# Another order for the first seven inner products of a float32 matrix kernel

## The chip, the cores and the metric

The kernel runs on one core of a Trainium2 chip. The metric is the device time of one execution in microseconds (us). An instruction that the profile calls PE ran on TensorE, PEld is TensorE's weight load, DVE is VectorE, ACT is ScalarE, POOL is GpSimd, and SP is the queue from which the kernel issues its loads.

## What is computed

The inputs are float32: x is 2048 x 1024, the two parts of a Fourier matrix over the sequence are 2048 x 2048, the two over the hidden dimension 1024 x 1024, w1 is 1024 x 3584 and w2 is 3584 x 1024.

```python
g = sigmoid((x * gate_w).sum(-1, keepdims=True))
a = einsum("bsd,ed->bse", x, dft_hid_re)
b = einsum("bsd,ed->bse", x, dft_hid_im)
y = einsum("ts,bse->bte", dft_seq_re, a) - einsum("ts,bse->bte", dft_seq_im, b)
h = relu(einsum("bsd,df->bsf", x, w1) + b1) ** 2
out = g * y + (1 - g) * (einsum("bsf,fd->bsd", h, w2) + b2)
```

The change lies in the very first product of the first line with a matrix: x with the hidden Fourier matrix (`x_stage`).

## The kernel before, in words

**Float32 by three matmuls.** TensorE works on operands that are split in two: `hi` is the operand rounded by a copy on ScalarE (L220), `lo` is what is left, made by a subtraction on VectorE (L230). One float32 product is hi·hi + hi·lo + lo·hi, three matmuls (L306). A block is a tile of 128 partitions by 2 x 512 elements (512 KB).

**Seven products for eight, at two levels.** Every large product is cut into 2 x 2 blocks and done with seven products of sums of blocks instead of eight (`FACTORS`, `SUMS_L`, `SUMS_R`: left sums S1 to S4, right sums T1 to T4, each one `tensor_tensor` on VectorE, L172). In `x_stage`, five of the seven outer products are again done by seven inner ones (`twice`). In what follows l00 to l11 are the left inner blocks of the very first outer product, r00 to r11 the right ones. The inner products are 1 = l00·r00, 2 = l01·r10, 3 = S4·r11, 4 = l11·T4, 5 = S1·T1, 6 = S2·T2, 7 = S3·T3, with S1 = l10 + l11, T1 = r01 - r00, S2 = S1 - l00, T2 = r11 - T1, S3 = l00 - l10, T3 = r11 - r01, S4 = l01 - S2, T4 = r10 - T2. Each is one step: 24 matmuls, 12 for each of two result tiles.

**Where results go.** PSUM holds four tiles of 128 x 2 x 512, so two steps can hold accumulators at a time. Products 1, 6, 7 and 4 form `chain`, one pair of accumulators that goes on from product to product: after 1 ScalarE copies it out (`put`, L596), after 6 and after 7 VectorE adds it into the block where it belongs (`add`, L603), after 4 ScalarE copies it. Products 5 and 3 form `other`, the second pair. Product 2 (`last`) needs the result of product 1 added: before it starts, ScalarE copies that result from memory back into its accumulators (`prepare`, L293, two copies), and `put` copies the sum out. A matmul that goes on in an accumulator waits until the copy or the add that reads it is done.

**What sets the order.** A loop goes over all steps of the kernel. For each it first emits loads, then the finished `later` work, then sums and `hi` copies of operands that are needed within three steps (`SUMS`) and `lo` parts within two (`RESTS`), then the step's matmuls and what takes its results out. Operands are loaded and made in the order in which the steps need them. A list scheduler puts the instructions of each engine in their final order, the earlier emitted first among those that it takes to be ready; each engine then runs its own in that order.

In the very first outer product the inner order is 1, 5, 3, 6, 2, 7, 4, in all others 5, 1, 3, 6, 2, 7, 4. The operands of product 1 are loaded in pieces ahead of the loop, and 44 small matmuls (`WARM`) run while they land.

## Time and profile before

| | |
|---|---|
| median of 3 runs | 1891.17 us (1890.40 to 1892.99) |
| the profiled execution, its own time | 1888.96 us |
| its span, first to last instruction | 1886.9 us |
| PE busy | 1876.6 us (99%) |
| DVE busy | 1610.3 us (85%) |
| ACT busy | 1001.3 us (53%) |
| DMA | 442.93 MB, mean 235 GB/s |

Busy time is the union of an engine's instructions. In a timeline, a row gives the start from the span's beginning, the duration (of several merged instructions together, with their count), engine, line, operation, and out<-in by the names in the program; what stands in brackets is the idle time before it and what ended it. A matmul row is longer than the distance to the next one, since matmuls overlap.

### The profile page before, as it was taken

The page shows a single profiled execution, that of the slowest core. Times are in us where ns is not written, and L with a number is a line of the kernel's source. Part 1 is how long each engine was busy: PE and PEld are TensorE (multiplying, and loading weights), DVE is VectorE, ACT ScalarE, POOL GpSimd, SP SyncE. Part 2 cuts the span into 40 slices and gives each one's busy share as a digit, 9 for nine tenths or more (in the row PEclk, how much of TensorE's full clock was granted, in tenths as well). Part 3 has the DMA queues.
Part 4 walks back from the last instruction along what each step waited for, and adds up shares of the span by engine and source line. Part 5 has one row for each costly group of instructions (what it writes and reads, how often), then busy time and mean ns, then how long its engine had stood idle before and what let it go on. Part 6 is the DMA issues. An engine that isn't in the chain of part 4 may idle for free.

```text
span 1886.9 us, 21962 instructions
## 1 busy us (share of the span) xinstructions
PE 1876.6 (99%) x8288; PEld 1551.3 (82%) x8288; DVE 1610.3 (85%) x1543; ACT 1001.3 (53%) x1123; POOL 86.8 (5%) x161
## 2 busy tenths in 40 slices
PE   9999999999999999999999999999999999999998
PEld 7888888888888888888888888888888888888887
DVE  8997898599777998798896997989976997789882
ACT  6474564363343554455484797767954434264440
POOL 0000110000010000000000000000100001000000
PEclk9999999999999999999999999999999999999999
DMA  5732989339786489383551865628872887629971
GB/s 223 247 121 86 348 288 412 129 117 375 261 312 256 151 322 383 139 312 112 170 198 56 325 228 195 228 84 299 293 259 97 317 336 265 218 103 370 409 300 45
DMA packets 128425, 442.93 MB, mean 235 GB/s; under 512 B 14128, under 2 KB 23616, under 8 KB 128320
## 3 DMA queue, kind: packets, MB, share of 16 engines
q1 hardware_dynamic: 106416, 363.26, 53.0%
q0 software_dynamic: 21472, 77.61, 10.3%
q8 instruction: 65, 1.06, 0.2%
q10 hardware_dynamic: 432, 0.66, 0.1%
q14 instruction: 40, 0.33, 0.1%
HBM read 362.83 MB, written 78.65 MB: 234 GB/s over the span
## 4 chain that ended last, share of the span: by engine, by line
PE 97%; DVE 2%; ACT 0%; DMA 0%; issue 0%; SPq 0%; DVEq 0%; ACTq 0%
PE ps L306 97%; DVE lo L230 1%; DVE h L603 0%; DVE sum L172 0%; DMA raw<-in_w 0%; DVE o L818 0%; ACT u L596 0%; ACT hi L220 0%; DVE o L820 0%; DVE raw L172 0%; SPq L152 0%; DVEq L172 0%; DVEq L230 0%; ACTq L596 0%
## 5 line engine op out<-in xcount | busy, mean ns | idle before, releaser
L306 PE MATMUL ps<-hi 128*128 128x512 f32 x2328 | 905.7, 390 | 4.0 <-ACT hi L220 3.6
L306 PE MATMUL ps<-lo,hi 128*128 128x512 f32 x2328 | 905.3, 389 | 0.0
L306 PE MATMUL ps<-hi,lo 128*128 128x512 f32 x2328 | 904.2, 389 | 0.1
L220 ACT ACTIVATE hi<-raw 128x1024 fp32r<-128x1024 f32 (+2 forms) x413 | 420.6, 1037 | 399.0 <-DVE raw L172 274.1
L230 DVE TENSOR_TENSOR lo<-raw,hi 128x1024 fp32r<-128x1024 f32 (+2 forms) x413 | 484.5, 1199 | 57.5 <-ACT hi L220 31.3
L306 PEld LDWEIGHTS ps<-hi 128*128 128x128 f32 x2328 | 437.2, 188 | 95.9 <-ACT hi L220 4.2
L306 PEld LDWEIGHTS ps<-hi,lo 128*128 128x128 f32 x2328 | 437.1, 188 | 92.0 <-DVE lo L230 1.0
L306 PEld LDWEIGHTS ps<-lo,hi 128*128 128x128 f32 x2328 | 437.3, 188 | 91.0 <-DVE lo L230 0.4
L172 DVE TENSOR_TENSOR raw<-raw 128x1024 f32<-128x1024 f32 (+1 forms) x276 | 326.4, 1207 | 56.4 <-DMA raw<-in_ct 19.4
L220 ACT ACTIVATE hi<-sum 128x1024 fp32r<-128x1024 f32 (+1 forms) x172 | 176.1, 1036 | 184.8 <-DVE sum L172 151.2
L306 PE MATMUL ps<-hi,both 128*128 128x512 f32 x840 | 259.8, 389 | 0.0
L230 DVE TENSOR_TENSOR lo<-sum,hi 128x1024 fp32r<-128x1024 f32 (+1 forms) x172 | 203.3, 1198 | 32.9 <-PE ps L306 16.6
L306 PEld LDWEIGHTS ps<-hi,both 128*128 128x128 f32 x840 | 157.7, 188 | 33.8 <-ACT ps L293 0.7
L306 PE MATMUL ps<-lo,both 128*128 128x512 f32 x420 | 163.5, 389 | 0.0
L172 DVE TENSOR_TENSOR sum<-raw 128x1024 f32<-128x1024 f32 (+1 forms) x116 | 121.9, 1066 | 35.4 <-PE ps L306 28.1
L172 DVE TENSOR_TENSOR sum<-raw,sum 128x1024 f32<-128x1024 f32 (+2 forms) x87 | 96.8, 1119 | 12.0 <-PE ps L306 11.7
L603 DVE TENSOR_TENSOR h<-h,ps 128x1024 f32<-128x1024 f32 x92 | 98.2, 1086 | 9.6 <-ACT u L596 7.1
L596 ACT ACTIVATE u<-ps 128x1024 f32<-128x1024 f32 x76 | 71.9, 950 | 62.0 <-PE ps L306 54.3
L306 PEld LDWEIGHTS ps<-lo,both 128*128 128x128 f32 x420 | 78.8, 188 | 16.1
L293 ACT ACTIVATE ps<-u 128x1024 f32<-128x1024 f32 (+1 forms) x74 | 70.0, 953 | 22.2 <-DVE o L831 12.0
L700 ACT ACTIVATE h<-h,b1c 128x512 f32<-128x512 f32 x112 | 74.3, 712 | 6.3 <-DVE h L603 6.0
L220 ACT ACTIVATE both<-sum 128x512 fp32r<-128x512 f32 x60 | 37.1, 625 | 52.7 <-DVE sum L172 33.4
(61 smaller groups left out, 650.5 us busy)
## 6 DMA issues: line engine op xcount, KB each, us to landing
raw<-in_ct SPq DMA_DIRECT2D x151, 512.0 KB, 6.2
raw<-h SPq DMA_DIRECT2D x132, 512.0 KB, 7.3
raw<-in_x SPq DMA_DIRECT2D x107, 512.0 KB, 5.3
raw<-in_w SPq DMA_DIRECT2D x98, 512.0 KB, 6.3
raw<-ab SPq DMA_DIRECT2D x72, 512.0 KB, 6.8
h<-h POOLq DMA_DIRECT2D x48, 512.0 KB, 5.7
raw<-in_w1a SPq DMA_DIRECT2D x36, 512.0 KB, 5.0
ab<-ab POOLq DMA_DIRECT2D x32, 512.0 KB, 6.7
```

Of the source, the lines that this page charges most:

```text
L172: nc.vector.tensor_tensor(self.slot[:, k, c], src[0][:, k, c], src[1][:, k, c], op=self.op)
L220: nc.scalar.activation(self.hi[:, k, c], self.block.slot[:, k, c], AF.Copy)
L230: nc.vector.tensor_tensor(self.lo[:, k, c], self.block.slot[:, k, c], self.hi[:, k, c].bitcast(F32), op=SUB)
L293: nc.scalar.activation(t[:, :n, :], b.slot[:, at:at + n, :], AF.Copy, scale=self.sign)
L306: nc.tensor.matmul(self.ps[r // self.per][:, r % self.per, :], a[:, kk, r * P:(r + 1) * P], b[:, kk, :], start=self.at == 1 and kk + n == ...
L596: nc.scalar.activation(view(near.slot, k), view(ps, k), AF.Copy, scale=float(sign))
L603: nc.vector.tensor_tensor(view(near.slot, k), view((src or dst)[k].slot, k), view(ps, k), op=ADD if sign > 0 else SUB)
L700: nc.scalar.activation(dst.slot[:, k, :], (dst.slot if ps is None else ps)[:, k, :], AF.Relu, bias=b1c[:, tile0 + k:tile0 + k + 1])
```

## The change

In the very first outer product alone (`if not steps`), the inner order becomes 1, 2, 5, 3, 6, 7, 4. Product 2 no longer has product 1's result copied into its accumulators: ScalarE copies product 2 out to a tile of its own (`two`), and one step later (`JOIN`) VectorE adds that tile to product 1's result, in two instructions. All later outer products keep their order and their way with product 2.

```diff
-LATER = 3
+LATER, JOIN = 3, 1
...
+            def two(rp, ps):
+                k = 0, 0, rp
+                t = Near("u")
+                nc.scalar.activation(view(t.new(), k), view(ps, k), AF.Copy)
+
+                def join():
+                    add(new, k, t.slot)
+                    t.drop()
+
+                later.append((now[0] + JOIN, join))
+
-            if old and not onto_old:
+            if not steps:
+                last = Group(rows, 1, (two, 2, [new[0, 0, rp] for rp in range(2)]))
+            elif old and not onto_old:
                 last = Group(rows, 1, takes(False, 0, 0, ends))
             else:
                 last = Group(rows, 1, (lambda rp, ps: put(new, (0, 0, rp), ps, ends, sign), 0,
                                        [new[0, 0, rp] for rp in range(2)]),
                              onto=[new[0, 0, rp] for rp in range(2)], sign=sign)
-            begin = ((5, other), (1, chain))
-            for p2, group in (*(begin if steps else begin[::-1]), (3, other), (6, chain), (2, last), (7, chain),
-                              (4, chain)):
+            if steps:
+                turns = (5, other), (1, chain), (3, other), (6, chain), (2, last), (7, chain), (4, chain)
+            else:
+                turns = (1, chain), (2, last), (5, other), (3, other), (6, chain), (7, chain), (4, chain)
+            for p2, group in turns:
                 l_, r_ = FACTORS[p2]
                 step(l2.operand(l_, rows * P), r2.operand(r_), group)
```

## The prediction

> **What bounds the kernel now.** I read the page first, for where TensorE stands idle.

> ```profile
> span 1886.9 us, 21962 instructions
> PE 1876.6 (99%) x8288; PEld 1551.3 (82%) x8288; DVE 1610.3 (85%) x1543; ACT 1001.3 (53%) x1123; POOL 86.8 (5%) x161
> L306 PE MATMUL ps<-hi 128*128 128x512 f32 x2328 | 905.7, 390 | 4.0 <-ACT hi L220 3.6
> ```

> TensorE is busy for all but about 10 us, and of the idle time that its groups show, 3.6 us ended with a `hi` copy. Nearly all of that is at one place, the gap after product 1. The timeline of TensorE's first 20 us shows it, and the windows around it give the clock (PEclk is the third column from the end):

> ```profile
> 10.03 1.07 PE L306 MATMUL ps<-lo,hi 128*128 128x512 f32 x4
> 10.94 1.07 PE L306 MATMUL ps<-hi,lo 128*128 128x512 f32 x4
> 14.91 0.80 PE L306 MATMUL ps<-hi 128*128 128x512 f32 x1 [2.91 <-ACT hi L220]
> 18.38 0.39 PE L306 MATMUL ps<-hi 128*128 128x512 f32 x1
> 18.61 0.39 PE L306 MATMUL ps<-lo,hi 128*128 128x512 f32 x1
> ...
> 12.00:14.60 2.60, 0.00 (x1) 0.00 (x0) 2.60 (x4) 2.60 (x4) 0.00 (x0) 1.00 1.03 419
> 14.60:18.00 3.40, 3.09 (x7) 2.16 (x8) 3.40 (x4) 3.40 (x5) 0.00 (x0) 0.50 1.02 407
> 18.00:21.40 3.40, 3.40 (x17) 2.81 (x16) 3.40 (x4) 3.40 (x4) 0.00 (x0) 1.00 1.01 398
> ```

> Four matmuls take 10.94 - 10.03 = 0.91 us, 0.227 each, so a step of 24 takes 5.44. Product 1's last four start at 10.94; the next could start at 10.94 + 0.91 = 11.85 and starts at 14.91, 3.06 late. Its first eight then take until 18.38, 3.47 where 8 x 0.227 = 1.81 would do, since the granted clock is 0.50 from 14.6 to 18.0: another 1.66. The gap is worth 3.06 + 1.66 = **4.72 us**, and this is all that the change can win.

> What held product 5 back is read from the two engines that make its operands:

> ```profile
> 8.64 2.35 DVE L172 TENSOR_TENSOR sum<-raw 128x1024 f32<-128x1024 f32 x2
> 10.99 1.23 DVE L230 TENSOR_TENSOR lo<-sum,hi 128x1024 fp32r<-128x1024 f32 x1
> 12.13 1.22 DVE L172 TENSOR_TENSOR sum<-raw 128x1024 f32<-128x1024 f32 x1
> 13.80 1.06 ACT L220 ACTIVATE hi<-sum 128x1024 fp32r<-128x1024 f32 x1
> ```

> S1 is the sum at 12.13 (l11, its second block, is the fifth load); its `hi` ends at 14.86 and TensorE goes on. Product 2 needs no sum.

> Then I asked whether VectorE has room for TensorE to run earlier. From its first sum to 99 us it has none:

> ```profile
> 8.64:99.01 90.37, 87.46 (x379) 71.64 (x378) 89.28 (x80) 53.50 (x55) 4.43 (x8) 0.98 0.67 240
> ...
> DVE lo L230 <- ACT hi L220: 0.4, 1, 0.4
> DVE ab L603 <- PE ps L306: 0.4, 1, 0.4
> ```

> The third group is VectorE: busy 89.28 of 90.37 us, with two waits of 0.4. That alone could be work done ahead. The places where TensorE takes the result show whether it is:

> ```profile
> 80.48 1.22 DVE L603 TENSOR_TENSOR ab<-ab,ps 128x1024 f32<-128x1024 f32 x1
> 95.31 3.71 DVE L230 TENSOR_TENSOR lo<-sum,hi 128x1024 fp32r<-128x1024 f32 x3
> ...
> 81.85 0.62 PE L306 MATMUL ps<-hi 128*128 128x512 f32 x2
> 98.17 0.39 PE L306 MATMUL ps<-hi 128*128 128x512 f32 x1
> 99.30 0.39 PE L306 MATMUL ps<-hi,lo 128*128 128x512 f32 x1
> ```

> The add that frees an accumulator ends at 80.48 + 1.22 = 81.70 and the second matmul of the 81.85 row, the first into that accumulator, starts at 82.08: 0.4 to spare. The last of the three `lo` ends at 95.31 + 3.71 = 99.02 and the matmul that reads it starts at 99.30: **0.3 to spare**. Of the three, two belong to the next step and fill the time until the third one's `hi` is made; nothing else had been done ahead there. So at 99 us TensorE stands where VectorE's whole work since 8.64 lets it, and the early gap is paid for out of time that VectorE needs.

> **The change part by part.**

> *The start.* Product 2's blocks now take the third and fourth place among the loads. These two issues and what the DMA view says of each, and of the fifth:

> ```profile
> 2.60 0.44 SPq L152 DMA_DIRECT2D raw<-in_w  x1
> 3.08 0.97 SPq L152 DMA_DIRECT2D raw<-in_x  x2
> ...
> raw<-in_w SPq DMA_DIRECT2D x1, 512.0 KB, 5.7
> raw<-in_x SPq DMA_DIRECT2D x1, 512.0 KB, 6.5
> raw<-in_x SPq DMA_DIRECT2D x1, 512.0 KB, 8.0
> ```

> They land at 2.60 + 5.7 = 8.3 and 3.08 + 6.5 = 9.6, the fifth at about 3.55 + 8.0 = 11.5 (it is the second in the row at 3.08, half of its 0.97 later). ScalarE takes 1.06 and VectorE 1.22 for each: `hi` at 9.4 and 10.7, `lo` at 10.6 and 11.9. Product 2 can start at 11.85 with all but its third kind of matmul, and that comes 0.45 later. I count the whole 4.72 as won here. The same loads cost VectorE: its first instruction behind product 1's own moves from 8.64 to 9.4, and three of them end at 13.1 (T1 waits for the fifth load, 11.5, and for the two `lo`), where the `lo` at 10.99 ended at 12.2: **+0.9 for everything behind**.

> *The joins.* They are new `tensor_tensor`s of 128 x 1024 from two tiles in memory, the shape of the sums. In a queue without a gap such an instruction costs the distance between starts:

> ```profile
> 41.25 1.22 DVE L603 TENSOR_TENSOR u<-u,ps 128x1024 f32<-128x1024 f32 x1
> 42.39 1.22 DVE L230 TENSOR_TENSOR lo<-raw,hi 128x1024 fp32r<-128x1024 f32 x1
> 43.52 1.22 DVE L172 TENSOR_TENSOR sum<-sum,raw 128x1024 f32<-128x1024 f32 x1
> 44.66 1.22 DVE L603 TENSOR_TENSOR u<-u,ps 128x1024 f32<-128x1024 f32 x1
> ...
> 43.77 0.39 PE L306 MATMUL ps<-hi 128*128 128x512 f32 x1
> ...
> L293 ACT ACTIVATE ps<-u 128x1024 f32<-128x1024 f32 x2 | 2.1, 1026 | 0.0
> ```

> Three distances are 3.41, so 1.137 each and **+2.27** for two. ScalarE loses the two copies into PSUM, 2.1 us; product 2's copies out stay. ScalarE was busy 53.50 of the 90.37 us, so its gain is worth at most VectorE's one wait on it, 0.4. The other wait, on TensorE, goes too once VectorE is later: **-0.8** together. The joins themselves are waited for by nobody before the next outer product; what is queued behind them is every `lo` from product 6 on.

> *The order 6, 7, 4.* Product 2 stood between 6 and 7 and gave VectorE 5.44 us for the adds that free `chain`; now product 7 follows at once. Ahead of the first of these adds the code emits 23 VectorE instructions: the two `lo` of product 2, eight sums, ten `lo`, two joins and one sum of the next outer product. From 11.98 (the second `lo`'s end), the add is the 24th: 11.98 + 22 x 1.137 = 37.0. TensorE, 4.72 earlier, would want product 7 at 11.85 + 4 x 5.44 = 33.6. It waits 3.4. Product 7's own add, six instructions on, ends at 43.8, where product 7 would be done at 37.0 + 5.44 = 42.4: 1.4 more. Product 4 so starts at 43.8. The nearest row of before, the add that freed the same accumulator, is the one at 41.25; it ended at 42.5, and product 4 began in the row at 43.77. By 44 us the whole gain is given back.

> *From there to 99 us.* VectorE is later by 0.9 + 2.27 - 0.8 = 2.4, with the same work before it. TensorE meets it with 0.3 to spare: **2.4 - 0.3 = +2.1 us**. The ends: if the two `lo` that belong to the next step are moved behind the one waited for, 2.27 less, -0.2; if neither wait goes and VectorE loses one more 1.06 for a `hi` at the start, +4.0. I take +2.1, since the queue's order follows the same rule. Behind 99 us I count nothing: VectorE's share of the span is 85%, so it gets ahead again.

> *The clock.* A stop of 3.06 us was followed by 3.4 us at 0.50. The stop at product 7 is about as long, so it may cost up to 1.66 there; that is hidden, since VectorE sets the end anyhow. [...]

> The profiled execution would take 1888.96 + 2.1 = 1891.1. It lies 2.2 under the median; on the median's footing **1893.3 us**, 0.11% more. About 0.2%, 3.8 us, is what a measurement of this kernel can tell from no change, so this forecast counts as no change.

> **The rivals.** *Slower: VectorE comes to wait for TensorE.* The adds of products 6 and 7 stand in VectorE's queue at a fixed place. If TensorE is late for one (half clock after its stop), VectorE stands still with all `lo` behind it, for up to half a product, 2.72. Then the end moves by 2.1 + 2.72 = 4.8, 1896.0; with the half clock again after a second stop between 82 and 99 us 6.5, 1897.7. It decides once VectorE's waits on TensorE before 99 us pass 1.7 in sum. For it: 6, 7, 4 in a row and a stop of the length that halved the clock. Against: VectorE's only such wait before was 0.4.

> *Faster: VectorE's queue finds the room.* An order that puts the adds ahead of sums that are needed later would keep the start's gain: -4.72, 1886.4. Against it stands the row at 95.31: at 99 us nothing is ahead.

> *It doesn't do what it says.* If product 2's operands come late the gap stays; VectorE is still 2.4 later, and the time is the forecast's.

> **How the numbers follow.** Forecast 0.55, of which 0.10 above 3.8; slower rival 0.35, of which 0.02 below; faster rival 0.06, of which 0.05 beyond 3.8; no effect at the start 0.04. That gives faster 0.05, same 0.45 + 0.02 + 0.01 + 0.04 = 0.52, slower 0.43. The forecast's own range is 1891.0 to 1895.2. The range given reaches down to 1889.5 for the runs' own spread of 1.3 below and above, and up to 1898.0 for the slower rival; outside stay the faster rival and worse than 6.7.

> **What would show it.** Right: product 2 starts near 11.9 without a wait at a full clock; two joins of 1.2 between 20 and 30 us; TensorE waits on VectorE by 45 us for most of 4.7; VectorE busy as before to 99; the step that began at 98.17 begins near 100. Wrong: TensorE still ahead of the old times at 110 us, or waits of VectorE on TensorE.

## The result, and the profile after

| | before | after |
|---|---|---|
| median of 22 runs each | 1890.39 us | 1894.68 us |
| lowest and highest | 1889.34, 1892.99 | 1892.96, 1896.06 |
| after / before | | 1.0021 [1.0015, 1.0027] |
| the profiled execution, its own time | 1888.96 us | 1895.16 us |

The change costs about 4 us (0.21% of 1890.4; 2.8 to 5.1 by the interval), where +2.1 was forecast. The two profiled executions stand 6.2 us apart, since before's lies 1.4 under its median and after's 0.5 above. What follows explains the profiles, so some 2 us of their difference belongs to these two executions and not to the change.

To see where the time went I set each matmul of after against the one with the same number of before. The distance of their starts, after minus before, is called the shift below; negative means that after is ahead. It moves at few places:

| place | shift, us |
|---|---|
| product 2, once both kernels run at a full clock again | -4.8 |
| most of product 5 | -3.8 |
| most of product 3 | -3.0 |
| first matmul of product 7 (37.75 us) | -0.6 |
| product 4 (45 us) | +1.2 |
| the next outer product's matmul of 85.48 us | +3.6 |
| from 90 us on | +5.3 |
| end | +6.2 |

The gain comes, is gone by 38 us, and two losses follow. Between 90 us and the end little happens but a step of 0.8 at 690 us, where TensorE waits for one `lo`. It belongs to this execution: three of the kernels below have such a step of 0.7 to 1.0 near 285 us and none at 690. TensorE's timeline of the changed kernel:

```profile
10.83 1.07 PE L306 MATMUL ps<-hi,lo 128*128 128x512 f32 x4
11.74 0.39 PE L306 MATMUL ps<-hi 128*128 128x512 f32 x1
...
37.75 0.73 PE L306 MATMUL ps<-hi 128*128 128x512 f32 x2 [2.29 <-ACT hi L220]
...
85.48 0.73 PE L306 MATMUL ps<-hi 128*128 128x512 f32 x2 [2.28 <-ACT hi L220]
```

The row at 11.74 has no bracket: product 2 starts behind product 1 without a wait, and the stop of 2.91 us is gone. Two stops stand in its place, 2.29 us ahead of product 7 and 2.28 us at 85.48. The windows around them (PEclk is the third column from the end):

```profile
33.00:38.46 5.46, 3.17 (x14) 2.31 (x13) 5.46 (x6) 4.24 (x4) 0.00 (x0) 1.00 0.40 138
38.46:41.87 3.41, 3.41 (x10) 2.62 (x9) 2.68 (x3) 0.00 (x0) 0.00 (x0) 0.50 0.21 87
...
82.50:86.25 3.75, 1.47 (x7) 0.91 (x6) 3.75 (x4) 1.71 (x2) 0.49 (x1) 1.00 0.94 294
86.25:89.66 3.41, 3.41 (x9) 2.64 (x8) 3.41 (x4) 0.00 (x0) 0.57 (x2) 0.50 0.92 374
```

Each stop is followed by 3.41 us at a granted clock of 0.50, which costs TensorE 1.7 us. Before had one stop and one such stretch, after has two of each. VectorE's timeline of the changed kernel shows the joins, the adds of products 6 and 7, and what it does ahead of 85 us:

```profile
9.13 2.50 DVE L230 TENSOR_TENSOR lo<-raw,hi 128x1024 fp32r<-128x1024 f32 x2 [1.02 <-ACT hi L220]
11.54 3.49 DVE L172 TENSOR_TENSOR sum<-raw 128x1024 f32<-128x1024 f32 x3
...
21.77 1.22 DVE L603 TENSOR_TENSOR u<-u 128x1024 f32<-128x1024 f32 x1
...
24.04 1.22 DVE L603 TENSOR_TENSOR u<-u 128x1024 f32<-128x1024 f32 x1
...
36.53 1.21 DVE L603 TENSOR_TENSOR u<-u,ps 128x1024 f32<-128x1024 f32 x1
...
42.63 1.22 DVE L603 TENSOR_TENSOR u<-u,ps 128x1024 f32<-128x1024 f32 x1 [1.49 <-PE ps L306]
...
45.38 1.22 DVE L603 TENSOR_TENSOR u<-u,ps 128x1024 f32<-128x1024 f32 x1 [0.39 <-PE ps L306]
...
83.12 1.21 DVE L172 TENSOR_TENSOR sum<-raw 128x1024 f32<-128x1024 f32 x1
```

And the same chain at the second stop, in before (VectorE's sum, then ScalarE's `hi` of it):

```profile
79.35 1.22 DVE L172 TENSOR_TENSOR sum<-raw 128x1024 f32<-128x1024 f32 x1
...
80.60 1.06 ACT L220 ACTIVATE hi<-sum 128x1024 fp32r<-128x1024 f32 x1 [1.21 <-DVE sum L172]
```

ScalarE's row of the same `hi` in after:

```profile
84.37 1.06 ACT L220 ACTIVATE hi<-sum 128x1024 fp32r<-128x1024 f32 x1 [1.21 <-DVE sum L172]
```

In before that `hi` ended at 80.60 + 1.06 = 81.66 and the matmul in the row at 81.85 read it. In after the same sum starts at 83.12, 3.77 later, and the matmul at 85.48 is 3.63 later. The matmul starts 2.50 behind the sum's start in before and 2.36 in after: TensorE had 0.14 us to spare there and is later by the rest. So the second stop is VectorE's queue, though the bracket names ScalarE's `hi`.

VectorE's start, below, is its first three instructions behind product 1's own: two sums and a `lo` in before, which end at 12.21, and the two `lo` of product 2 and T1's sum in after, which end at 12.76. The windows from there to this sum say what the 3.77 consist of. The first line is of before, the second of after; VectorE is the third group:

```profile
12.21:79.35 67.14, 64.44 (x277) 52.94 (x278) 66.17 (x60) 41.57 (x43) 2.30 (x4) 0.97 0.59 214
```

```profile
12.76:83.12 70.36, 67.31 (x285) 53.74 (x283) 68.35 (x62) 39.09 (x40) 2.30 (x4) 0.98 0.57 208
DVE u L603 <- PE ps L306: 1.9, 2, 1.5
```

The start is 0.55 later (12.76 - 12.21). VectorE is busy 68.35 - 66.17 = 2.18 longer, with 62 instructions instead of 60: the two joins. It stands idle 70.36 - 68.35 = 2.01 instead of 67.14 - 66.17 = 0.97, so 1.04 more, and the second line, of its waits, says for what: 1.9 us in two waits for TensorE, at 42.63 and 45.38. Together 0.55 + 2.18 + 1.04 = 3.77.

### The profile page after: what moved, and what is told of

Same layout as the page of the kernel before. It is cut to its first block, busy times and chain, and to the rows that moved or that the text cites. A ratio compares the mean times of both kernels' runs of the same rounds, so it can differ in the third digit from the quotient of the medians.

```text
span 1893.1 us, 21965 instructions
## 1 busy us (share of the span) xinstructions
PE 1880.0 (99%) x8288; PEld 1552.4 (82%) x8288; DVE 1612.0 (85%) x1545; ACT 999.4 (53%) x1121; POOL 86.8 (5%) x161
## 3 DMA queue, kind: packets, MB, share of 16 engines
q8 instruction: 65, 1.06, 0.2%
## 4 chain that ended last, share of the span: by engine, by line
PE 94%; DVE 4%; DMA 1%; issue 0%; ACT 0%; SPq 0%; DVEq 0%; ACTq 0%
PE ps L306 94%; DVE lo L230 1%; DVE sum L172 1%; DVE h L603 0%; DVE raw L172 0%; DMA raw<-in_ct 0%; DMA b2c<-in_b 0%; DMA raw<-in_x 0%; DVE ab L603 0%; ACT hi L220 0%; SPq L152 0%; DVE o L833 0%; DVE o L835 0%; DVE u L603 0%; ACT u L596 0%
## 5 line engine op out<-in xcount | busy, mean ns | idle before, releaser
L306 PE MATMUL ps<-hi 128*128 128x512 f32 x2328 | 906.4, 390 | 5.8 <-ACT hi L220 5.2
L306 PE MATMUL ps<-hi,lo 128*128 128x512 f32 x2328 | 905.7, 390 | 1.1 <-DVE lo L230 1.0
L306 PE MATMUL ps<-lo,hi 128*128 128x512 f32 x2328 | 905.9, 390 | 0.0
L220 ACT ACTIVATE hi<-raw 128x1024 fp32r<-128x1024 f32 (+2 forms) x413 | 421.0, 1038 | 405.2 <-DVE raw L172 276.5
L230 DVE TENSOR_TENSOR lo<-raw,hi 128x1024 fp32r<-128x1024 f32 (+2 forms) x413 | 483.4, 1195 | 60.7 <-ACT hi L220 33.1
L306 PEld LDWEIGHTS ps<-hi 128*128 128x128 f32 x2328 | 437.5, 188 | 99.2 <-ACT hi L220 7.0
L306 PEld LDWEIGHTS ps<-hi,lo 128*128 128x128 f32 x2328 | 437.5, 188 | 93.4 <-DVE lo L230 2.4
L306 PEld LDWEIGHTS ps<-lo,hi 128*128 128x128 f32 x2328 | 437.7, 188 | 91.6 <-DVE lo L230 0.4
L172 DVE TENSOR_TENSOR raw<-raw 128x1024 f32<-128x1024 f32 (+1 forms) x276 | 325.4, 1202 | 58.8 <-DMA raw<-in_ct 15.7
L220 ACT ACTIVATE hi<-sum 128x1024 fp32r<-128x1024 f32 (+1 forms) x172 | 176.1, 1036 | 180.9 <-DVE sum L172 149.1
L306 PE MATMUL ps<-hi,both 128*128 128x512 f32 x840 | 259.8, 389 | 0.0
L230 DVE TENSOR_TENSOR lo<-sum,hi 128x1024 fp32r<-128x1024 f32 (+1 forms) x172 | 203.1, 1194 | 31.0 <-ACT hi L220 16.9
L306 PEld LDWEIGHTS ps<-hi,both 128*128 128x128 f32 x840 | 157.7, 188 | 33.9 <-ACT ps L293 0.7
L306 PE MATMUL ps<-lo,both 128*128 128x512 f32 x420 | 163.5, 389 | 0.0
L172 DVE TENSOR_TENSOR sum<-raw 128x1024 f32<-128x1024 f32 (+1 forms) x116 | 121.4, 1062 | 33.9 <-PE ps L306 27.7
L172 DVE TENSOR_TENSOR sum<-raw,sum 128x1024 f32<-128x1024 f32 (+2 forms) x87 | 96.3, 1113 | 12.0 <-PE ps L306 11.7
L603 DVE TENSOR_TENSOR h<-h,ps 128x1024 f32<-128x1024 f32 x92 | 97.9, 1081 | 10.1 <-ACT u L596 7.5
L306 PEld LDWEIGHTS ps<-lo,both 128*128 128x128 f32 x420 | 78.8, 188 | 16.1
L293 ACT ACTIVATE ps<-u 128x1024 f32<-128x1024 f32 (+1 forms) x72 | 68.0, 951 | 21.6 <-DVE o L846 11.9
L220 ACT ACTIVATE both<-sum 128x512 fp32r<-128x512 f32 x60 | 37.1, 624 | 50.8 <-DVE sum L172 32.3
## 6 DMA issues: line engine op xcount, KB each, us to landing
raw<-in_ct SPq DMA_DIRECT2D x151, 512.0 KB, 6.4
raw<-h SPq DMA_DIRECT2D x132, 512.0 KB, 7.6
raw<-in_x SPq DMA_DIRECT2D x107, 512.0 KB, 5.1
raw<-in_w SPq DMA_DIRECT2D x98, 512.0 KB, 6.5
raw<-ab SPq DMA_DIRECT2D x72, 512.0 KB, 7.2
h<-h POOLq DMA_DIRECT2D x48, 512.0 KB, 5.9
raw<-in_w1a SPq DMA_DIRECT2D x36, 512.0 KB, 5.2
ab<-ab POOLq DMA_DIRECT2D x32, 512.0 KB, 6.1
```

Of the source, the lines that this page charges most:

```text
L172: nc.vector.tensor_tensor(self.slot[:, k, c], src[0][:, k, c], src[1][:, k, c], op=self.op)
L220: nc.scalar.activation(self.hi[:, k, c], self.block.slot[:, k, c], AF.Copy)
L230: nc.vector.tensor_tensor(self.lo[:, k, c], self.block.slot[:, k, c], self.hi[:, k, c].bitcast(F32), op=SUB)
L293: nc.scalar.activation(t[:, :n, :], b.slot[:, at:at + n, :], AF.Copy, scale=self.sign)
L306: nc.tensor.matmul(self.ps[r // self.per][:, r % self.per, :], a[:, kk, r * P:(r + 1) * P], b[:, kk, :], start=self.at == 1 and kk + n == ...
L603: nc.vector.tensor_tensor(view(near.slot, k), view((src or dst)[k].slot, k), view(ps, k), op=ADD if sign > 0 else SUB)
```

## The experiments

Each was run in five rounds beside the kernel before on the same chip; the ratio is to that. A trace shows one execution, up to 2.4 us from the median of its kernel (`e2_join_alone`), so places are compared and not ends. "The shift at 82 us" is that of the matmul that starts at 81.85 in before and at 85.48 in after. The theories that the expectations name by letters:

- **Q**: VectorE's queue decides when TensorE can run up to about 82 us. What the start wins, TensorE waits off; what VectorE gets more, TensorE pays.
- **S**: the early gap is worth what it shows, and a change that fills it without new costs keeps it.
- **O**: the order 6, 7, 4 is what costs. **J**: the joins cost only through their place in the queue.
- **C**: a half-clock stretch behind a stop adds to the time. **V**: it is hidden, since VectorE sets the end anyhow.

| kernel | median, us | before, us | ratio |
|---|---|---|---|
| `e1_warm_gap` | 1889.77 | 1890.58 | 0.9996 [0.9987, 1.0005] |
| `e2_join_alone` | 1892.77 | 1890.58 | 1.0014 [1.0005, 1.0023] |
| `e3_order_alone` | 1890.80 | 1890.58 | 1.0003 [0.9995, 1.0012] |
| `e4_join_gpsimd` | 1893.81 | 1890.58 | 1.0016 [1.0007, 1.0024] |
| `e5_apart` | 1893.29 | 1890.52 | 1.0018 [1.0009, 1.0026] |
| `e6_twice_the_joins` | 1894.80 | 1890.52 | 1.0024 [1.0014, 1.0035] |
| `e7_join_late` | 1893.97 | 1890.52 | 1.0019 [1.0010, 1.0028] |
| `e9_relief` | 1887.47 | 1890.52 | 0.9985 [0.9976, 0.9994] |
| `e10_keep_clock` | 1892.27 | 1890.32 | 1.0011 [1.0002, 1.0020] |
| `e11_seed` | 1890.96 | 1890.32 | 1.0005 [0.9996, 1.0014] |
| `e12_seed_clock` | 1891.85 | 1890.32 | 1.0007 [0.9998, 1.0016] |

The intervals reach 1.6 to 2 us to each side, so several of these ratios don't differ from one another by themselves; the shifts in the traces, place by place, carry the verdicts. One reading holds for all of them: in the ten kernels that stop at 82 us, after among them, that matmul starts 2.36 or 2.37 behind the start of VectorE's sum, whether the sum starts at 79.62 (e11) or at 85.37 (e6). TensorE goes on there when VectorE's sum lets it.

**`e1_warm_gap`: the gap's clock alone.** The kernel before, with 48 small matmuls on ones in the gap, so that TensorE isn't idle there.

```diff
-WARM = 44
+WARM, GAP = 44, 48
...
             group.run(st, mv, by_part=i == 0)
+            if i == 0:
+                fill = steps[1][2].ps[1]
+                for _ in range(GAP):
+                    nc.tensor.matmul(fill[:, 0, :P], ones, ones, start=True, stop=True)
```

> The kernel before, with 48 small bf16 matmuls into a still unused accumulator between product 1 and product 5, so that TensorE isn't idle in the gap of 3.06 us. Theory Q (up to 99 us VectorE's queue sets when TensorE can go on): the granted clock stays at 1.00 behind the gap, TensorE is 1.66 us earlier for a while, and meets VectorE at 82 to 99 us, where it had 0.3 to 0.4 to spare: end at -0.4 to 0 us against before. Rival S (the gap is worth what it costs, VectorE has room): -1.7 us.

Measured: no difference from before; the interval, -2.5 to +0.9 us, holds Q's forecast and S's, and the trace has to decide. The windows over the gap and behind it, in this kernel, and two of its matmul rows:

```profile
12.00:14.60 2.60, 2.49 (x43) 2.31 (x42) 2.60 (x3) 2.60 (x4) 0.00 (x0) 1.00 1.06 424
14.60:18.00 3.40, 1.95 (x7) 1.33 (x8) 3.40 (x4) 3.40 (x4) 0.00 (x0) 1.00 1.00 400
...
15.43 0.50 PE L306 MATMUL ps<-hi 128*128 128x512 f32 x1 [0.94 <-ACT hi L220]
...
17.25 0.51 PE L306 MATMUL ps<-hi,lo 128*128 128x512 f32 x1 [0.62 <-DVE lo L230]
```

The clock stays at 1.00, where before had 0.50 from 14.6 to 18.0. The matmuls are no earlier for it: they wait 0.94 for `hi` and 0.62 for `lo`, and at 99 us the shift is -0.08. So nothing was won that Q and S could differ on. Of the 4.72 that the gap was worth in the prediction, the 1.66 of the half clock were not to be had: the operands come no faster.

**`e3_order_alone`: the new order without the joins.** The inner order of after, product 2 started on product 1's result as before did, no `two`. (The start's matmuls on ones go over both of product 2's accumulators. The output has a relative error of 0.21, which the author puts down to product 1's result not being whole in product 2's sum; the work is the same in number and size.)

```diff
-            if not steps:
-                last = Group(rows, 1, (two, 2, [new[0, 0, rp] for rp in range(2)]))
-            elif old and not onto_old:
+            if old and not onto_old:
                 last = Group(rows, 1, takes(False, 0, 0, ends))
...
```

> [...] Product 2 waits for a copy out and a copy in of product 1's result and starts near 13.9 us instead of 11.7. Q: VectorE has no instruction more, so the end is 2.3 us under the changed kernel's: +1.5 to +2.5 us against before, what is left being VectorE's later start and its waits on TensorE. Rival O: as the changed kernel, +4 us or more. Rival S: -2.7 us.

Measured: no difference from before. Product 2 waits for the copies into its accumulators:

```profile
15.21 0.79 PE L306 MATMUL ps<-hi 128*128 128x512 f32 x1 [3.44 <-ACT ps L293]
...
83.07 0.74 PE L306 MATMUL ps<-hi 128*128 128x512 f32 x2 [0.83 <-ACT hi L220]
```

So the gap comes back (3.44), half clock with it (0.52 from 15.0 to 18.4); at 82 us the shift is only +1.2 and behind it the clock stays full (1.00 from 82 to 92). Products 6, 7 and 4 in a row cost nothing by themselves as long as TensorE comes to them no earlier: O falls as the main cause. S was not put to the test, since the gap was not filled, and Q's +1.5 to +2.5 is met only by the upper part of the interval (-0.9 to +2.3).

**`e2_join_alone`: the joins without the new order.**

```diff
-                turns = (1, chain), (2, last), (5, other), (3, other), (6, chain), (7, chain), (4, chain)
+                turns = (1, chain), (5, other), (3, other), (6, chain), (2, last), (7, chain), (4, chain)
```

> The old order 1, 5, 3, 6, 2, 7, 4, but with product 2 copied out and joined by two VectorE adds: the joins without the new order. Q: two instructions of 1.137 us more in VectorE's queue, less 0.3 to spare and less one or both of its waits of 0.4: +1.2 to +2.0 us against before. Rival S: 0, the joins are hidden. Rival O (the back-to-back order 6, 7, 4 is the whole cost): 0.

Measured: slower, 1.0014; the median is 2.2 us over before's, where Q had +1.2 to +2.0 and S and O had 0. The profiled execution took 1895.17, 2.4 over the median. In it the half clock in the early gap lasted 6.83 us by the clock records instead of 3.41, TensorE was 2.1 late from 24 us on, and VectorE waited 2.5 us for two `hi`. The shift is +4.3 at 82 us and +6.0 behind it. The second stop, and the window behind it:

```profile
86.13 0.73 PE L306 MATMUL ps<-hi 128*128 128x512 f32 x2 [2.06 <-ACT hi L220]
...
87.40:90.80 3.40, 3.40 (x10) 2.64 (x9) 3.40 (x4) 0.00 (x0) 0.53 (x1) 0.51 0.92 375
```

Four of the eleven executions show a mean granted clock of 0.997, as this one does, and their median is 1894.98; five show 0.999, and theirs is 1892.09. So the trace is of the costlier kind; the five are 1.5 over before's median, as Q forecast.

With the joins and the old order the kernel loses 2.6 us by the ratio, after 4.0, and the intervals overlap; with the new order and no joins it loses nothing that can be measured. S had after 4.7 better than this kernel, which never filled the gap: S falls. Q, by which VectorE's queue holds both kernels at 82 us, fits both.

**`e4_join_gpsimd`: the joins on GpSimd.**

```diff
-                    add(new, k, t.slot)
+                    nc.gpsimd.tensor_tensor(view(new[k].slot, k), view(new[k].slot, k), view(t.slot, k), op=ADD)
```

> The changed kernel with the two joins on GpSimd instead of VectorE. Q: 2.3 us off VectorE's queue before 99 us, so the end is about 2 us under the changed kernel's: +1.5 to +2.5 us against before. Rival O: as the changed kernel, +4 us. Rival S: the whole gain of the start, -4.7 us.

Measured: 1.0016, shift +4.9 at 82 us; taking the joins off VectorE's queue didn't bring the 2 us that Q forecast. GpSimd's timeline and VectorE's show why:

```profile
16.79 2.42 POOL L651 TENSOR_TENSOR u<-u 128x1024 f32<-128x1024 f32 x1 [16.34 <-ACT u L648]
...
16.89 3.40 DVE L172 TENSOR_TENSOR sum<-sum,raw 128x1024 f32<-128x1024 f32 x1
20.21 1.21 DVE L230 TENSOR_TENSOR lo<-sum,hi 128x1024 fp32r<-128x1024 f32 x1
```

The sum that began 0.10 behind GpSimd's instruction took 3.40 instead of 1.22: it ended at 20.29, 1.08 after GpSimd's end at 19.21, which looks, by these rows alone (the profile's spans of GpSimd are rough), as if it had stood still until GpSimd was done. At the second join, 2.44 us on GpSimd from 22.37, the two sums from 22.48 took 4.54 where the two from 37.16 took 2.35. VectorE loses 2.2 us to each join there, more than the 1.137 of doing it itself.

**`e5_apart`: products 6 and 7 apart.** The order 1, 2, 5, 6, 3, 7, 4; ScalarE takes 6 out of its accumulators and VectorE adds 3 instead, so that product 7 no longer follows on 6 and its add; 4 still follows on 7. Joins as in after.

```diff
...
-                turns = (1, chain), (2, last), (5, other), (3, other), (6, chain), (7, chain), (4, chain)
+                turns = (1, chain), (2, last), (5, other), (6, chain), (3, other), (7, chain), (4, chain)
```

> The changed kernel with product 3 between 6 and 7 (1, 2, 5, 6, 3, 7, 4): ScalarE takes product 6 out, VectorE adds product 3's result, so VectorE has as many instructions as in the changed kernel, joins included, but product 7 no longer follows on product 6. Theory Q (VectorE's queue sets TensorE's time up to 99 us): the stop before product 7 and VectorE's waits of 1.9 us on TensorE go, the work stays: +1 to +2.5 us against before. Rival O (the back-to-back order is the cost): most of the start's gain is kept, -3 us or better.

Measured: 1.0018, by the medians +2.8, a little above Q's range and far from O's. TensorE keeps 3 us of the gain until 82 us, with no stop at product 7, and then gives it back at once, in one stop of 4.70 us (TensorE's timeline), with 6.8 us of half clock across it (clock records of the trace, from 81.4):

```profile
83.71 1.22 PE L306 MATMUL ps<-hi 128*128 128x512 f32 x2 [4.70 <-ACT hi L220]
...
82.00:92.00 10.00, 8.29 (x27) 6.69 (x28) 9.91 (x10) 3.18 (x3) 1.06 (x2) 0.69 0.84 302
```

The shift is +1.9 behind the stop and +4.1 behind the half clock. VectorE's waits for TensorE, 1.9 in after, are 0.2 here, and the shift at the stop is lower by about as much: 3.6 - 1.9 = 1.7. So the three in a row do cost VectorE those waits, but the gain of the start is lost without them too.

**`e7_join_late`: the joins four steps later.**

```diff
-LATER, JOIN = 3, 1
+LATER, JOIN = 3, 5
```

> The changed kernel with JOIN = 5: the joins come behind the adds of products 6 and 7 in VectorE's queue, and still ahead of 66 us, where they are first needed. Q: the stop before product 7 is some 2.3 us shorter, but the work up to 82 us is the same, so the end is the changed kernel's: +2.5 to +4.5 us against before. Rival J (the joins cost only because they stand ahead of these adds): 2.3 us under the changed kernel, +2 us or less.

Measured: 1.0019; TensorE is 1.8 ahead up to 82 us, then +2.8, and +5.4 behind the half clock (0.50 from 85.0 to 88.4), as in after. J had +2 us or less and is left with the very end of the interval (+1.9 to +5.3); the joins cost about the same at both places that were tried.

**`e6_twice_the_joins`: the dose.** Each join is followed by one more add of the same size.

```diff
                     add(new, k, t.slot)
+                    nc.vector.tensor_tensor(view(t.slot, k), view(t.slot, k), view(t.slot, k), op=ADD)
...
```

> The changed kernel with each join followed by one more VectorE add of the same shape, into the tile that is dropped (its result is not used): two instructions of 1.137 us more early in VectorE's queue. Q: 2.3 us on top of the changed kernel, +6 to +7 us against before. Rivals S and O: as the changed kernel, +4 us.

Measured: 1.0024 (eight runs), 4.3 us by the medians. By its time alone this kernel is where S and O had it (+4) and not where Q had it (+6 to +7); the trace says why. VectorE's sum ahead of the second stop, at 83.12 in after, and the last three of its start, at 11.54 in after, stand in this kernel's timeline of VectorE at

```profile
12.08 3.49 DVE L172 TENSOR_TENSOR sum<-raw 128x1024 f32<-128x1024 f32 x3
...
47.95 1.22 DVE L603 TENSOR_TENSOR u<-u,ps 128x1024 f32<-128x1024 f32 x1 [0.60 <-PE ps L306]
...
85.37 1.22 DVE L172 TENSOR_TENSOR sum<-raw 128x1024 f32<-128x1024 f32 x1
```

The sum is 2.25 later, and the matmul that waits for it too (shift +5.9 for +3.6). That two adds of 1.137 give 2.27 is partly luck: this execution's start is 0.54 later than after's, and VectorE waits 0.6 for TensorE and 0.4 for a `hi` instead of 1.9 for TensorE, 0.9 less. The dose arrives within some 0.4 us, then, and Q asks for all of it. TensorE's stop behind:

```profile
87.73 0.73 PE L306 MATMUL ps<-hi 128*128 128x512 f32 x2 [1.74 <-ACT hi L220]
...
82.00:92.00 10.00, 8.26 (x37) 6.53 (x36) 10.00 (x10) 3.18 (x3) 1.60 (x3) 1.00 0.93 338
```

The stop of 1.74 left the clock at 1.00, so the end is only 0.6 later than after's, not 2.25. What VectorE gets to do is paid by TensorE at 82 us; what the clock does on top is a matter of its own.

**`e9_relief`: VectorE relieved.** After, with twelve instructions taken off VectorE: both joins are left out, and ten sums are copies of their first term by ScalarE.

```diff
+                if self.op and (self.need in (5, 6) or self.need in (14, 15, 16) and self.room() == 2):
+                    nc.scalar.activation(self.slot[:, k, c], src[0][:, k, c], AF.Copy)
-                if self.op:
+                elif self.op:
...
-                    add(new, k, t.slot)
                     t.drop()
```

> The changed kernel with 12 instructions taken off VectorE in the first 92 us, to see what TensorE does when VectorE has room. Left out of the computation: the two joins (product 2 of the first outer product is not added), and the additions of ten sums (S3, T3, T4 of the first outer product, seven outer sums that are needed between 81 and 99 us), which become ScalarE copies of their first block. 12 x 1.137 = 13.6 us less in VectorE's queue. Q: no stop before product 7 nor at 82 us, TensorE keeps what it has after product 3: -4 to -2.5 us against before. If VectorE does not bind: as the changed kernel, +4 us.

Measured: 0.9985, the only one under before, with work left out. The longest of TensorE's waits between 11 and 110 us, and a window over the place of the second stop:

```profile
PE ps L308 <- ACT u L650: 1.0, 1, 1.0
...
82.00:92.00 10.00, 10.00 (x46) 8.29 (x45) 10.00 (x10) 4.93 (x6) 1.07 (x2) 1.00 0.98 331
```

No stop at product 7, none at 82 us, no half clock (1.00 from 11 to 92 us); the shift is -2.3 from product 3 to 100 us and between -2.1 and -2.4 from there on. Once VectorE has room, what is left of the start's gain stays. This is Q's strongest case. It also shows that the start was not worth 4.72: of 4.2 won at product 2, 2.0 are lost by the end of product 3, half of it in the wait above, for ScalarE's copy of product 2's result (1.0). In after 1.8 of 4.8 go in the same stretch, in short waits for `lo` and for copies out of accumulators.

**`e10_keep_clock`: the half clock alone.** After, with 30 and 24 matmuls on ones ahead of product 7 and ahead of the step at 85 us.

```diff
+FILL = {5: (7, 30), 13: (14, 24)}
...
+            if i in FILL:
+                spare = steps[FILL[i][0]][2]
+                spare.prepare()
+                for _ in range(FILL[i][1]):
+                    nc.tensor.matmul(spare.ps[1][:, 0, :P], ones, ones, start=True, stop=True)
```

> The changed kernel with small bf16 matmuls into a free accumulator ahead of the two places where TensorE stops: 30 before product 7 and 24 before the last product of the second outer product (82 us of before). They fill the stops, so that the granted clock should stay at 1.00. Theory C (each stop that halves the clock adds up to 1.7 us on top of what VectorE sets, and makes VectorE wait for TensorE): 2 to 3.4 us under the changed kernel, +0.5 to +2 us against before. Theory V (VectorE alone sets the end, the half clock is hidden, as the prediction had it): as the changed kernel, +4 us.

Measured: 1.0011, 1.95 us over before, where after was 4.29 over it on its chip. The window at 82 us and VectorE's waits for TensorE between 11 and 86 us:

```profile
82.00:92.00 10.00, 9.07 (x58) 7.40 (x57) 10.00 (x10) 2.89 (x4) 1.06 (x2) 1.00 0.81 297
...
DVE u L604 <- PE ps L307: 0.3, 1, 0.3
```

The clock stays at 1.00, VectorE waits 0.3 for TensorE instead of 1.9 (and 1.1 once for a `hi`), and the shift behind the second stop is 3.0 instead of 5.3. So the half clock, which cost nothing in before's gap by e1, cost about 2 us in after (2.3 by the medians, and as much by these shifts): C holds there and V falls. The intervals of the two ratios overlap, so the size is not sharper than that. After's own executions agree: two stretches of 3.41 us bring the mean granted clock of an execution to 0.998 or less, so the twelve of 22 that show 0.999 had one at most. Their median is 1893.86 us, that of the other ten, among them the profiled one, 1894.87. The traces show two ways of the cost. Behind product 7 it makes TensorE late for VectorE's adds. Behind 85 us nobody else is late any more, and it goes straight into the end.

**`e11_seed` and `e12_seed_clock`: a version without joins.** The order of e5; ScalarE copies product 1's accumulators straight into product 2's, so that neither the joins nor the copies by way of memory are needed. e12 adds 30 matmuls on ones ahead of the step at 82 us.

```diff
+        def seed(self, ps):
+            self.pools.append(banks.popleft())
+            self.ps.append(self.pools[-1].tile([P, 2, 512], F32, name="ps", tag="ps"))
+            nc.scalar.activation(flat(self.ps[-1]), flat(ps), AF.Copy)
...
+                turns = (1, chain), (2, last), (5, other), (6, chain), (3, other), (7, chain), (4, chain)
...
```

> The order 1, 2, 5, 6, 3, 7, 4 without joins: ScalarE copies product 1's result straight from its accumulators into those of product 2, which adds onto it (product 1 is no longer copied to memory; the warm-up matmuls write all four banks of product 2's accumulators once). VectorE has two instructions less than in the kernel with product 3 between 6 and 7, where its limit at 82 us was 1.9 us behind the old time, so 0.4 us ahead of it. Theory Q: the end is that limit plus a half-clock stretch of up to 2 us, since the stop at 82 us is over 3 us long: -0.5 to +1.5 us against before. Rival S: -4 us.

> The kernel before this one with 30 small bf16 matmuls into a free accumulator at the stop at 82 us, so that the clock stays. Theory Q with C: VectorE's limit alone, -1.5 to 0 us against before, and 1 to 2 us under the kernel without these matmuls. Theory V: no difference from it.

Measured: 1.0005 and 1.0007, neither to be told from before nor from each other. TensorE's timeline of e11:

```profile
81.98 0.73 PE L311 MATMUL ps<-hi 128*128 128x512 f32 x2 [1.74 <-ACT hi L220]
```

TensorE comes 1.8 us ahead of before, waits 1.74 and goes on 0.3 behind before's time. Nothing is added to VectorE, nothing is won: S's -4 falls, and Q's range holds the result, though the stop is shorter than the 3 us that it named. e11's trace shows no half clock (1.00 from 11 to 92 us), so e12 had none to remove; it came out 0.9 us above e11 where Q with C had it 1 to 2 under, and it says nothing for or against C. No version that I ran does all the work and beats before.

## Why the prediction was right and wrong

**Right: the start and the meeting.** Product 2 starts without a wait at 11.74 (11.85 was worked out), at a full clock (1.00 until 38.46). The joins cost 2.18 us of VectorE (2.27). TensorE gives the whole gain back by 45 us. VectorE's queue decides until the next outer product; e9 and e6 show it from both sides. Nothing of the change stands behind 99 us.

**"I count the whole 4.72 as won here"** was too much. e1 shows that the half clock in it was free, and e9 that with VectorE relieved 2.3 us of the start are kept. It didn't move the forecast, since all of it was given back.

**"+0.9 for everything behind"** measured 0.55: T1's sum ended at 12.76, not 13.1.

**"-0.8 together", the first step that failed.** VectorE's idle time was to go, since it would be late everywhere. It rose by 1.04. The price was that of a VectorE that waits for nobody, but the add of product 7 waits for a product that starts late and runs at half clock: 37.75 + 24 x 0.227 is 43.2 at a full clock, and the half clock puts 1.7 on that. This is the slower rival's mechanism. It decided "once VectorE's waits on TensorE before 99 us pass 1.7", and they came to 1.9. The 2.72 that it gave as their bound was too much.

**The stop at product 7**: 2.29 us, 3.4 were worked out; the add was nearly where it was put (it ended at 36.53 + 1.21 = 37.74, for 37.0), and TensorE came at 35.07 + 0.23 = 35.3, not at 33.6, having waited for operands and copies in products 5 and 3. Product 4 started at 45.18, not 43.8, since it stood behind product 7 at half clock.

**"That is hidden, since VectorE sets the end anyhow", the second step that failed.** The clock's 1.66 us was left out of the sum. Behind product 7 it came back through VectorE's waits. The second stop, which the forecast itself implied by putting TensorE 2.1 late, halved the clock again, past the point where VectorE limits anything, and cost 1.7 in full. The stop that VectorE's queue caused there, 2.28 us long, took the shift from +1.2 to +3.6, and the half clock behind it from +3.6 to +5.3.

**"With 0.3 to spare" at 99 us**: the meeting place was 82 us, and the row quoted for it had less to spare than the 0.4 read off it. The accumulator's add wasn't the last thing there, but the `hi` of the sum at 79.35, which ended at 81.66 for a start at 81.85. The forecast thought 2.4 later minus 0.3; the trace shows 3.77 minus 0.14, and 1.7 of half clock: 5.3. e10, with the clock kept, has +3.0 behind the same place, not far from the +2.1 of the forecast, and 1.95 in its medians.

**In sum**: the mechanism forecast, plus the light form of the slower rival, whose mark, waits of VectorE on TensorE, the prediction itself names as a sign that it is wrong. The step that began at 98.17 was to begin near 100; it begins at 103.5 in the profiled execution. The 4.0 of the ratio is 1.9 above the forecast and nearer to that rival's 4.8; e10 and the granted clocks of after's executions put most of it down to the clock, as far as the intervals let one say. The median, 1894.68, lies within the range. That it is only 1.4 above the 1893.3 is partly luck: the three runs on which the forecast stands have a median 0.8 above that of the 22. Two sums of the prediction are a little off, and nothing hangs on them: 0.9 + 2.27 + 1.06 - 0.3 is 3.9 and not 4.0, and 1891.0 less 1.3 is 1889.7 and not 1889.5.

## What to carry to other kernels

The early stop of the bottleneck engine was worth only what the next busy engine could follow, here none of 4.72 us in after and 2.3 in e9: elsewhere too, take the place where that engine meets the bottleneck again, and count every instruction that it gets more by the distance between starts. If a change moves a stop instead of removing it, price the clock at the new place too, and ask there whether anything else is still late enough to hide it. The same half clock was free in before's gap, where the operands came no faster, and cost 1.7 us at 85 us; in e2's trace, where it lasted twice as long in the gap, it was not free there either.

## What the runs showed of the hardware

**The clock fell after stops shorter than the stretch that followed.** The half-clock stretches behind a stop were 3.41 us or 6.83 us long, by the clock records of all kernels. The stops ahead of them were 2.06 us (e2), 2.28 and 2.29 (after) and up to 4.70 (e5). Length alone didn't decide: e4 stopped as long as after and kept its clock, by TensorE's timeline and the window behind it:

```profile
86.76 0.73 PE L306 MATMUL ps<-hi 128*128 128x512 f32 x2 [2.29 <-ACT hi L220]
...
86.00:90.00 4.00, 3.24 (x14) 2.71 (x15) 4.00 (x4) 0.71 (x1) 1.07 (x2) 1.00 0.88 346
```

The places of the changes say more. In each of the 13 traces, all changes of the clock stand whole multiples of 3.413 us apart (in before the full clock lasts 1867.09 us, 547 of them). So every trace can be cut into windows of that length, and TensorE's idle time in each taken from its matmul rows, whose ends the profile models, up to the last of them:

| granted clock in a window, and behind it | windows | TensorE idle in the window, us |
|---|---|---|
| 1.00, then 0.50 | 10 | 2.06 to 3.11 |
| 1.00, then 1.00 | 7128 | at most 1.74 |
| 0.50, then 1.00 | 10 | at most 0.32 |
| 0.50, then 0.50 | 5 | 0.50 to 2.30 |

**A VectorE sum beside a GpSimd add took longer**: in e4 a sum that began 0.10 us behind a GpSimd add of 2.42 us took 3.40 us, where the sums at 30.35 and 32.62, with GpSimd idle, took 1.21.
